# Backward dense stages of a four-layer attention gradient: transposes moved from DMA to TensorE, dq moved, TensorE order set by hand

## The chip, the cores and the metric

The kernel runs on one core of a Trainium2 chip. The metric is the device time of one execution in microseconds, as the median of several executions. Profiles are of one execution each; the two main ones span 3151.3 us (before) and 2894.6 us (after).

## The reference

Forward and gradient of four layers, A B A B, on x of 2048 tokens by 640. A is linear attention with 32 heads of 20; B is softmax attention over a sliding window of 256. Every layer is `x + layer(layernorm(x))`. Outputs: the result, the gradient of x, and the gradients of the four weights (two layers share each).

```python
def _A_ref(x, wqkv, wo):
    q, k, v = split(x @ wqkv)                     # 32 heads of 20
    pq, pk = phi(q), phi(k)                       # where(t > 0, t + 1, exp(t)) + 1e-6
    kv = einsum("bhsd,bhse->bhde", pk, v); z = sum(pk over s)
    return merge(einsum(pq, kv) / (einsum(pq, z) + 1e-6)) @ wo
def _B_ref(x, wqkv, wo):
    p = softmax(mask(q k^T * 20**-0.5))           # 0 <= i - j < 256
    return merge(p v) @ wo
_out, _vjp = jax.vjp(_f, A_x, A_wqkv, A_wo, B_wqkv, B_wo)
return (_out, *_vjp(grad_out))
```
(Names shortened, cuts not marked one by one.)

## The kernel before

The program goes through these stages: forward; dO of layer 3 ("first stage"); attention backward of layer 3; B-to-A (gradient through layer 3's wqkv and layernorm, then dO of layer 2); A-to-B (dq, dk, dv of layer 2, its wqkv and layernorm, then dO of layer 1); attention backward of layer 1; B-to-A and A-to-B again for layers 1 and 0; weight gradients. Tokens go in 16 tiles of 128. `dh` is the large product of a tile (30 matmuls of 320 columns in two halves). The names: `car` holds the gradient of x, `gT` is its transposed tile, which the dO product multiplies with `WoT`; `dqkvT` (after the change `dqT` and `dkvT`) is the transposed gradient of q, k and v, which `dh` multiplies with `WT`; `dNT`, `vT` and `pkT` are the transposed tiles from which dq, dk and dv are made, with small block matrices such as `mbdT`; `dOT` is the transposed output of the dO product for attention. Each product needs its left operand transposed, and before the change nearly all those transposes were DMA transposes issued from SyncE:

```python
def tr(self, out, in_):
    self.nc.sync.dma_start_transpose(out=out, in_=in_)

def load_gT(self, l, tt, pw):
    gT = pw.tile([P, self.DT, P], BF, name="gT")
    self.tr(gT, self.car[:, tt, :])               # car: the gradient of x, all tiles
    self.dma(self.g_d[l][:, tt, :], self.car[:, tt, :])
    return gT

def seg_A_to_B(self, l, acc, dNT):
    ...
    for tt in range(self.TT + 2):
        if tt < self.TT:
            dq[tt] = pw.tile([P, self.QT], BF, name="dqkv_t", bufs=3)
            self.A_dqkv(l, tt, dNT, mats, dq[tt], pw, pps)
        t = tt - 1
        if 0 <= t < self.TT:
            dT = pw.tile([P, self.QTT, P], BF, name="dqkvT")
            self.tr(dT, dq[t])
            self.dma(self.dqkv_d[l][:, t, :], dq.pop(t))
            self.dh(l, t, dT, WT, pw, pps)        # updates car[t]
            ...
        t = tt - 2
        if l > 0 and 0 <= t < self.TT:
            gT = self.load_gT(l - 1, t, pw)
            self.B_do(l - 1, t, gT, WoT, ...)
```

The builder orders each engine's instructions itself, starting from the order of the program; inside `manual_schedule` it keeps the program's order on the engines that are named. Before the change only attention backward did that.

The softmax here doesn't subtract the row's maximum and nothing guards it: scores larger than these inputs give would overflow.

## Time and profile before

| | before |
|---|---|
| median, all its runs beside the change | 3141.5 us (3125.9 to 3158.7, 4 runs); 3156.4 us when the prediction was made |
| five dense stages, with their starts and ends | 1022 us |
| the two attention backwards | 394 + 412 us |
| forward, weight gradients | 902 us, 421 us |

The first part of the page: busy time of each engine and its share of the span. No engine is near full over the whole.

```profile
PE 2248.5 (71%) x22944; PEld 1197.3 (38%) x22944; DVE 1383.5 (44%) x2994; ACT 1066.0 (34%) x2009; POOL 773.2 (25%) x1290
```

Windows cut the span into stretches. The columns are: start and end, length, busy time (and count) of TensorE's matmuls, of its weight loads, of VectorE, ScalarE and GpSimd, the granted TensorE clock, the DMA engines' share, GB/s. I cut at the first and last instruction of `dh` in each dense stage. These are, in order: the first stage, the start of B-to-A (from the last matmul of attention to the first dh), the loop of B-to-A, its end with the start of A-to-B, the loop of layer 2, and, for layer 0, the loop and the step to the weight gradients.

```profile
core 0: us, PE busy (x) PEld busy (x) DVE busy (x) ACT busy (x) POOL busy (x), PEclk, DMA share, GB/s
902.30:1009.60 107.30, 37.29 (x166) 19.71 (x167) 47.26 (x129) 0.00 (x0) 11.40 (x19) 0.63 0.96 213
1403.40:1444.40 41.00, 0.29 (x12) 0.13 (x4) 0.00 (x0) 0.37 (x1) 7.96 (x13) 0.50 1.01 221
1444.40:1586.30 141.90, 106.61 (x739) 72.55 (x739) 91.25 (x229) 16.35 (x62) 25.73 (x55) 0.86 0.62 130
1586.30:1648.60 62.30, 14.00 (x108) 8.08 (x106) 17.32 (x47) 2.03 (x6) 12.39 (x16) 0.61 0.86 174
1648.60:1842.50 193.90, 144.41 (x927) 87.20 (x928) 117.95 (x338) 26.44 (x89) 28.27 (x52) 0.82 0.98 213
...
2530.40:2690.80 160.40, 116.11 (x787) 71.08 (x788) 80.03 (x233) 26.90 (x90) 24.01 (x38) 0.83 0.80 169
2690.80:2730.40 39.60, 0.32 (x3) 0.02 (x1) 2.69 (x7) 0.53 (x2) 0.00 (x0) 0.56 1.13 194
```

TensorE is busy for 107 of 142 us in the loop of B-to-A and 116 of 160 us in layer 0, at a clock of 0.83 to 0.86, while ScalarE is busy for only 16 and 27 us of them. The DMA engines are busy nearly all the time in the first stage and in layer 2 (0.96 and 0.98), not in B-to-A (0.62).

Who TensorE waited for in the loop of layer 2, and then in that of layer 0 (total us, times, longest):

```profile
PE d L565 <- DMA dqkvT<-dqkv_t: 32.6, 6, 12.7
PE d L516 <- DMA gT<-car: 26.3, 7, 6.8
```
```profile
PE d L565 <- DMA dqkvT<-dqkv_t: 60.4, 9, 16.1
```

The chain of waits through layer 0, in order of time (start, length, what; L565 is dh):

```profile
2562.44 9.59 DMA dqkvT<-dqkv_t
2572.07 3.17 PE d L565 x12
2575.24 9.76 DMA dqkvT<-dqkv_t
2585.05 6.63 PE d L565 x30
2593.41 0.58 PE d L622 x9
```

The chain alternates between a DMA transpose of 7 to 16 us and the product that it feeds. Thirty matmuls right after such a wait take up to 6.6 us. Without a wait before them they take 4.1 to 4.2.

### The profile page before, as it was taken

Reading aid. Unit: us, or ns where it says so; the run is one execution under the profiler, and the core shown is the slowest. Engines: PE = TensorE matmul, PEld = TensorE weight load, DVE = VectorE, ACT = ScalarE, POOL = GpSimd, SP = SyncE. Lnnn points to the kernel's source line nnn. Section 1 sums busy time; section 2 is a strip of 40 time slices with the busy share of each in tenths; the row PEclk is TensorE's granted clock in tenths of the full one; section 3 lists DMA queues with packets and bytes.
Section 4 is the critical chain, followed back from the end, with each engine's and each line's share of the span. In section 5 each row is a group of like instructions: output and inputs, shape, how many; then the busy total and the mean of one; then the engine's idle time right before and its main releaser. Section 6 shows DMA issues by size and latency. Waiting matters only on the chain. (4 is left out here: it accounts for less than half of the span.)

```text
span 3151.3 us, 57835 instructions
## 1 busy us (share of the span) xinstructions
PE 2248.5 (71%) x22944; PEld 1197.3 (38%) x22944; DVE 1383.5 (44%) x2994; ACT 1066.0 (34%) x2009; POOL 773.2 (25%) x1290
## 2 busy tenths in 40 slices
PE   7598986699862977774737648776937466497796
PEld 5345544355431322233524423222324344244344
DVE  6344544344233765553736646565726445100000
ACT  4166764277621655540101116554601011000000
POOL 0134442255431433331211113332312111000000
PEclk9789987798755555557868865555568678798898
DMA  6789873989769999998679979999986688954624
GB/s 202 209 161 192 177 176 86 201 180 177 178 162 234 244 201 195 202 185 158 135 162 210 228 197 219 209 194 182 189 169 144 150 162 175 192 119 148 222 78 147
DMA packets 1195024, 563.54 MB, mean 179 GB/s; under 512 B 1036544, under 2 KB 1157376, under 8 KB 1193728
## 3 DMA queue, kind: packets, MB, share of 16 engines
q1 hardware_dynamic: 927488, 245.73, 49.2%
q10 hardware_dynamic: 252544, 261.66, 28.4%
q0 software_dynamic: 14720, 52.44, 6.4%
q8 instruction: 180, 2.95, 0.4%
q14 instruction: 92, 0.75, 0.1%
HBM read 178.65 MB, written 151.13 MB: 105 GB/s over the span
## 5 line engine op out<-in xcount | busy, mean ns | idle before, releaser
L732 DVE TENSOR_TENSOR ds<-sp,e 128x768 bf16<-128x768 f32 (+2 forms) x512 | 460.4, 907 | 319.6 <-PE sp L699 268.5
L713 ACT ACTIVATE e<-sp 128x768 bf16<-128x768 f32 (+2 forms) x512 | 390.2, 774 | 301.7 <-PE sp L699 283.1
L344 ACT ACTIVATE e<-s 128x768 bf16<-128x768 f32 (+2 forms) x512 | 374.0, 774 | 142.2 <-PE s L342 95.9
L565 PEld LDWEIGHTS <-dqkvT 128*128 128x128 bf16 x1920 | 205.8, 109 | 285.5 <-DMA dqkvT<-dqkv_t 99.1
L699 PE MATMUL sp<-KT,QT 32*128 32x384 bf16 (+2 forms) x1024 | 242.6, 477 | 84.0 <-ACT e L713 29.7
L717 POOL TENSOR_SCALAR_AFFINE_SELECT e<-e 128x512 bf16<-128x512 bf16 x256 | 162.5, 635 | 546.3 <-ACT e L713 296.1
L699 PE MATMUL sp<-VT,dOT 32*128 32x384 bf16 (+2 forms) x1024 | 245.1, 470 | 45.9 <-DVE ds L732 29.1
L347 POOL TENSOR_SCALAR_AFFINE_SELECT e<-e 128x512 bf16<-128x512 bf16 x256 | 162.7, 636 | 410.0 <-ACT e L344 371.0
L567 ACT ACTIVATE dh_junk<-d 128x320 bf16<-128x320 f32 x128 | 55.9, 437 | 564.5 <-PE d L565 553.5
L895 DVE CAST wg_r<-wg 128x480 bf16<-128x480 f32 (+1 forms) x36 | 21.7, 602 | 432.3 <-PE wg L891 432.3
L342 PE MATMUL s<-ring 32*128 32x128 bf16 x2880 | 167.9, 236 | 25.6 <-ACT e L344 24.2
L774 PE MATMUL acc<-dsT,ksl 128*32 128x128 bf16 x2880 | 125.8, 305 | 81.3 <-DMA dsT<-ds 79.7
L897 ACT CAST wg_r<-wg 128x480 bf16<-128x480 f32 (+1 forms) x24 | 12.3, 514 | 440.0 <-PE wg L891 440.0
L516 PEld LDWEIGHTS <-gT 128*128 128x128 bf16 x640 | 71.2, 117 | 208.5 <-DMA gT<-car 160.5
L350 POOL TENSOR_SCALAR_AFFINE_SELECT e<-e 128x512 bf16<-128x512 bf16 x224 | 143.3, 640 | 0.0
L721 POOL TENSOR_SCALAR_AFFINE_SELECT e<-e 128x512 bf16<-128x512 bf16 x224 | 142.2, 635 | 0.0
L342 PEld LDWEIGHTS <-ring 32*128 32x128 bf16 x2880 | 83.9, 98 | 134.6 <-issue 127.7
L699 PEld LDWEIGHTS <-dOT 32*128 32x128 bf16 x1024 | 77.7, 99 | 150.1 <-issue 145.4
L699 PEld LDWEIGHTS <-QT 32*128 32x128 bf16 x1024 | 54.8, 100 | 203.6 <-issue 201.4
L216 PEld LDWEIGHTS <-ln_hnT 128*128 128x128 bf16 x960 | 95.9, 106 | 93.0 <-DMA ln_hnT<-ln_hn 36.2
L203 DVE TENSOR_TENSOR car<-d,car 128x320 bf16<-128x320 f32 x128 | 62.2, 486 | 156.7 <-PE d L201 156.0
L363 PEld LDWEIGHTS <-e 128*128 128x128 bf16 x2880 | 103.5, 98 | 67.0 <-POOL e L350 37.9
(587 smaller groups left out, 4076.2 us busy)
## 6 DMA issues: line engine op xcount, KB each, us to landing
qkvT_128<-ring ACTq DMA_DIRECT2D x16, 768.0 KB
qkvT_132<-ring ACTq DMA_DIRECT2D x16, 768.0 KB
dqkvT_118<-dqkvT_g SPq DMA_DIRECT2D x96, 80.0 KB
dqkvT<-dqkvT_118 POOLq DMA_DIRECT2D x4, 1920.0 KB, 18.7
dqkv_116<-dqkv_t ACTq DMA_DIRECT2D x16, 480.0 KB
dqkvT_117<-dqkvT_g SPq DMA_DIRECT2D x96, 80.0 KB
dqkvT<-dqkvT_117 POOLq DMA_DIRECT2D x4, 1920.0 KB, 17.0
dqkv_115<-dqkv_t ACTq DMA_DIRECT2D x16, 480.0 KB
```

Of the source, the lines that this page charges most:

```text
L342: nc.tensor.matmul(ps[:, j, i * P:(i + 1) * P], lhsT=ring[r0:r0 + HP, G + g, kt * P:(kt + 1) * P], rhs=ring[r0:r0 + HP, g, qs], start=True ...
L344: nc.scalar.activation(ev[:, 2 * half:2 * half + 2], ps[:, :, 0:nkt * P].rearrange("p h (i q) -> p h i q", q=P), ACT.Exp, scale=self.c_att)
L347: nc.gpsimd.affine_select(out=ev[:, :, nkt - 1, :], in_=ev[:, :, nkt - 1, :], compare_op=ALU.is_ge, fill=0.0, base=0, pattern=[[0, 4], [1, ...
L350: nc.gpsimd.affine_select(out=ev[:, :, 0, :], in_=ev[:, :, 0, :], compare_op=ALU.is_ge, fill=0.0, base=-1, pattern=[[0, 4], [-1, P]], chan ...
L363: nc.tensor.matmul(ov[:, (g % 4) * 4 + hh, :], lhsT=ev[:, hh, i, :], rhs=slabs[(k0 + i) % len(slabs)][:, c0:c0 + DH + 1], start=(i == 0), ...
L565: nc.tensor.matmul(ps, lhsT=dT[:, k, :], rhs=WT[:, k, cs], start=(k == 0), stop=(k == self.QTT - 1))
L699: nc.tensor.matmul(ps[:, j, 0:nkt * P], lhsT=slabs[g][ta][r0:r0 + HP, b * P:(b + 1) * P], rhs=slabs[g][tb][r0:r0 + HP, k0 * P:(k0 + nkt) * P],
L713: nc.scalar.activation(ev[:, 2 * half:2 * half + 2], ps[:, :, 0:nkt * P].rearrange("p h (i k) -> p h i k", k=P), ACT.Exp, scale=c_att)
L717: nc.gpsimd.affine_select(out=ev[:, :, nkt - 1, :], in_=ev[:, :, nkt - 1, :], compare_op=ALU.is_ge, fill=0.0, base=0, pattern=[[0, 4], [-1 ...
L721: nc.gpsimd.affine_select(out=ev[:, :, 0, :], in_=ev[:, :, 0, :], compare_op=ALU.is_ge, fill=0.0, base=-1, pattern=[[0, 4], [1, P]], chann ...
L732: nc.vector.tensor_tensor(out=dv[:, hs], in0=ps[:, :, 0:nkt * P].rearrange("p h (i k) -> p h i k", k=P), in1=ev[:, hs], op=ALU.mult)
L774: nc.tensor.matmul(acc[HP * hh:HP * (hh + 1), j * P:(j + 1) * P], lhsT=tok("k", g, k0 + i, hh), rhs=dsT[:, hh * nkt + i, :], start=(i == 0 ...
```

## The change

The intent: take the DMA transposes out of the loops by making them on TensorE (matmul with the identity into PSUM, then one ScalarE copy for up to eight blocks); move dq of the A layers from A-to-B to B-to-A, beside its dO; take work off VectorE (t2 to ScalarE, the product for do_s to GpSimd, the slab scaling folded into rinv); issue stores from SyncE; and set TensorE's order by hand so that each transpose stands whole tiles, or half a tile's dh, away from what it waits for. The core of the diff, with cuts marked:

```diff
+    def flip(self, out, blocks, pps):
+        nc = self.nc
+        n = len(blocks)
+        tp = pps.tile([P, 8 * P], BF, name="d")
+        for i, b in enumerate(blocks):
+            nc.tensor.transpose(tp[:, i * P:(i + 1) * P], b, self.ident)
+        nc.scalar.copy(out, tp[:, 0:n * P].rearrange("p (k t) -> p k t", t=P))
...
-        nc.vector.tensor_mul(t, dst, o)
+        nc.gpsimd.tensor_mul(self.hv(t), dst, self.hv(o))
...
-        nc.vector.tensor_scalar(out=t2, in0=hn, scalar1=ab[:, 1:2], scalar2=ab[:, 0:1], op0=ALU.mult, op1=ALU.add)
+        nc.scalar.activation(t2, hn, ACT.Identity, bias=ab[:, 0:1], scale=ab[:, 1:2])
...
     def seg_B_to_A
+            self.dma(mbdT, self.sv[la]["mbdT"])
+            st.enter_context(self.tc.manual_schedule(engines={mybir.EngineType.PE}))
...                                     # dh(i,0), flip g(i-1), dh(i,1), flip dN(i-2), dO(i-1), dq(i-2), flip dq(i-3)
     def seg_A_to_B
+            st.enter_context(self.tc.manual_schedule(engines={mybir.EngineType.PE}))
+            for i in range(-2, TT + 1):
+                    self.dh(l, t, 0, dTs, WT, S, pw, pps)                       # t = i
+                    gT[t] = self.flip_g(l - 1, t, pw, pps)                      # t = i - 1
+                    dkv[t] = self.A_dkv(l, t, lds.pop(t), mats, pw, pps)        # t = i + 1
+                    self.dh(l, t, 1, dTs, WT, S, pw, pps)                       # t = i
+                        self.flip(dkvT[t][:, h * DT:(h + 1) * DT, :], ...)      # t = i + 1, two of them
+                    lds[t] = self.A_loads(l, t, pw, pps)                        # t = i + 2, flips pk
+                    self.B_flip(l - 1, t, pps)                                  # t = i - 2
+                    self.B_do(l - 1, t, gT.pop(t), WoT, pw, pps)                # t = i - 1
```

The transposed weights WT and WoT at the start of each stage, and vT, stay DMA transposes.

## The prediction

> **What bounds the kernel now.** No engine does over the whole span: the first part of the page has TensorE busy 71%, VectorE 44%, ScalarE 34%. I cut the span of 3151 us into stages with the windows view. The change touches five backward dense stages, 934 us in all: dO of layer 3 (77 us), B-to-A (192 us, twice), A-to-B for layer 2 (262 us) and layer 0 (211 us). Forward (905 us), both attention backwards (426 and 430 us) and weight gradients (456 us) keep their code. In those five stages the chain of waits alternates between TensorE and DMA transposes: gT<-car 2.7 to 9 us a wait, dqkvT<-dqkv_t 7 to 16 us a wait. In sum TensorE idles for them 62 us in layer 0, 62 us in layer 2, 41 and 36 us in B-to-A, 37 us in the first stage. ScalarE is nearly idle there (17 us of 192, 29 us of 262). The granted clock is 0.68 to 0.79. A run of 30 dh matmuls takes 4.2 us when TensorE has been kept going, 5.5 to 6.6 us just after such a wait; the Trainium skill ("TensorE: Matmul & The Clock Gate", The HAM clock gate) says that an idle window halves the clock, and these durations agree.
>
> **What changes.** Removed: nearly all per-tile DMA transposes but vT (1.2 us of issue each, 5 us for dqkvT, 2.7 us or more to land), those of dmbdT, one pq reload, and a VectorE pass each for t2 (0.60 us), do_o (0.82) and the slab scaling (0.32). Added: TensorE transposes of 128x128, which I estimate at 0.06 us each at full clock from the 0.064 us of the block-diagonal matmuls of similar width: 16 a tile in B-to-A, 28 in layer 2, 15 in layer 0, 13 in the first stage. Each group needs a ScalarE copy; from 437 ns for 320 and 774 ns for 768 elements I estimate 0.68 us for 640 and 0.97 us for 1024. dq moves into B-to-A (about 0.75 us TensorE and 0.97 us VectorE a tile), which is already full.
>
> Work per tile at full clock, estimated (TensorE / VectorE / ScalarE), against the present pace:
> - first: 2.1 / 2.3 / 1.7 us; now 4.1; expected 3.0
> - B-to-A: 8.2 / 7.0 / 4.2; now 9.4; expected 9.2
> - A-to-B layer 2: 8.3 / 7.0 / 6.9; now 14.1; expected 9.8
> - A-to-B layer 0: 6.2 / 4.8 / 5.0; now 10.1; expected 8.0
>
> **On the critical path.** Times 16 tiles: about 18 + 2x3 + 69 + 34 = 127 us. The start of each A-to-B stage (30 and 48 us) loses the dmbdT transposes: 10 us each; the WT load stays. Starts of B-to-A (41 us wait for WT) stay. Sum 147 us, and 9 more for a warmer clock: **3000 us**, 2930 to 3065 eight times in ten. Faster by over 2%: 0.88; within 2%: 0.10; slower: 0.02.
>
> **What would show it.** Windows: B-to-A near 185 us, layer 2 near 185, layer 0 near 165, first stage near 55; the others within 5 us of now. Waits: gT and dqkvT gone from TensorE's list, shorter ones on ScalarE copies instead. Granted clock above 0.85 in these stages. ScalarE busy more than doubled there.
>
> **What would make it wrong.** The hand-made order is strict: dh of the next tile needs the dkvT copies; if ScalarE does t2 or other copies first, TensorE stalls 2 us or more a tile in layer 0. Stores moved to SyncE wait in order ahead of vT's transposes, which could starve dkv. GpSimd's do_o multiply lies between TensorE and the slab flip. If the transposes don't hold the clock up (same page, PE-mode transpose: they don't count as busy; untested here), the first stage gains little. If none bites, 2930.

## The result, and the profile after

The change takes 2896.6 us (2870.6 to 2898.1, 4 runs), against 3141.5 us: a ratio of 0.920, 95% interval 0.912 to 0.928. A ratio here is the mean time of one kernel's fast runs over that of the other's of the same rounds, so not quite the ratio of the medians. The direction was right; the time lies well below the predicted range (2930 to 3065), and the gain was 245 us, not 156.

The same windows after (the first stage; start and loop of B-to-A; its end with the start of A-to-B; loop of layer 2; then layer 0 and the step to the weight gradients):

```profile
908.80:978.10 69.30, 40.36 (x370) 29.54 (x369) 45.47 (x81) 26.98 (x32) 35.20 (x37) 0.82 0.73 198
1392.60:1433.40 40.80, 0.40 (x13) 0.23 (x6) 1.68 (x2) 0.37 (x1) 13.63 (x20) 0.50 1.00 246
1433.40:1553.80 120.40, 117.04 (x1057) 83.20 (x1057) 91.76 (x239) 55.33 (x117) 42.30 (x54) 0.98 0.40 129
1553.80:1596.00 42.20, 22.51 (x193) 16.23 (x192) 14.84 (x40) 12.93 (x21) 14.30 (x15) 0.66 0.57 132
1596.00:1727.80 131.80, 128.99 (x1231) 95.33 (x1229) 93.78 (x251) 87.81 (x181) 41.59 (x55) 0.99 0.65 177
...
2351.00:2448.90 97.90, 97.88 (x913) 70.49 (x910) 61.42 (x181) 65.54 (x153) 14.56 (x27) 0.99 0.51 146
2448.90:2473.10 24.20, 0.25 (x3) 0.03 (x2) 2.14 (x7) 1.45 (x3) 0.00 (x0) 0.62 1.03 323
```

In the three loops TensorE is now busy 97 to 100% of the time at a clock of 0.98 or more. It is the bound, and it has hardly a gap. The lists of waits say the same: in the loops of B-to-A they hold, beside the wait for WT before the first dh, 3.2 and 3.9 us for VectorE; in the loop of layer 0 TensorE's list is empty, and in that of layer 2 it holds one line:

```profile
PE d L144 <- DVE car L596: 2.6, 3, 1.2
```

The chain through layer 0 is TensorE alone (L614 products with the block matrices, L581 dh, L144 the transposes), 6.23 us a tile:

```profile
2366.94 0.58 PE d L614 x9
2367.52 2.04 PE d L581 x15
2369.56 0.84 PE d L144 x15
2370.40 2.04 PE d L581 x15
2373.17 0.58 PE d L614 x9
```

The first dh half starts at 2367.52 here and again at 2373.75: that is the tile time. The 15 transposes take 0.84 us, 0.056 us each. ScalarE did fit its copies in between; the third line below is both copies of dkvT, and t2 (L595) comes after them, which was the order that the prediction had doubted:

```profile
2394.58 0.44 ACT L583 ACTIVATE dh_junk<-d 128x320 bf16<-128x320 f32 x1 [1.50 <-PE d L581]
2394.91 0.19 ACT L583 ACTIVATION_READ_ACCUMULATOR dh_junk<-d 128x1 f32 x1
2395.00 1.28 ACT L145 COPY dkvT<-d 128x640 bf16<-128x640 bf16 x2
2396.16 0.72 ACT L145 COPY pkT<-d 128x640 bf16<-128x640 bf16 x1
2396.74 0.95 ACT L595 ACTIVATE dh_t_35695<-hn_ld,dh_ab 128x640 f32<-128x640 bf16 x1
```

In B-to-A the chain shows the start of each tile's dO product (L538):

```profile
2242.53 1.36 PE d L538 x10
...
2249.86 1.36 PE d L538 x10
...
2264.71 1.36 PE d L538 x10
...
2273.80 1.36 PE d L538 x10
```

A tile takes 7.33 us (2242.53 to 2249.86), and 9.09 us where the band products of four tiles stand in it (2264.71 to 2273.80), so these cost 1.76 us in four tiles.

What remains in the dense stages is at their starts. TensorE's list over the whole execution still has WT, which comes by DMA transpose:

```profile
PE d L581 <- DMA WT_32780<-in_B_wqkv_dram: 40.8, 1, 40.8
PE d L581 <- DMA WT_21469<-in_B_wqkv_dram: 40.4, 1, 40.4
```

Where the time went, in us, by the two profiles (cut at the same TensorE instructions in both; "A-to-B" counts to the first matmul of the stage after it):

| part | before | after | gained | predicted gain |
|---|---|---|---|---|
| first stage | 107.3 | 69.3 | 38 | 18 |
| starts of B-to-A (two) | 85.7 | 82.0 | 4 | 0 |
| loops of B-to-A (two) | 278.9 | 242.1 | 37 | 6 |
| ends of B-to-A with starts of A-to-B (two) | 123.3 | 81.6 | 42 | 20 |
| layer 2, loop and end | 227.1 | 157.4 | 70 | 69 |
| layer 0, loop | 160.4 | 97.9 | 63 | 34 |
| layer 0 to the first weight-gradient matmul | 39.6 | 24.2 | 15 | 0 |
| sum of these | 1022.3 | 754.5 | 268 | 147 |

Forward, attention and weight gradients together are 11 us longer in this one profile. Attention backward of layer 3 alone lay anywhere between 379 and 415 us in the fast profiles (424 in a slow one), in kernels whose attention code is the same, so single profiles are compared by the dense stages, and whole times by the medians. The predicted gains add to 147 us; the prediction then took 9 more for a warmer clock.

### The profile page after: what moved, and what is told of

It is laid out like the page before. It is cut to its first block, busy times and chain, and to the rows that moved or that the text cites. A ratio compares the mean times of both kernels' runs of the same rounds, so it can differ in the third digit from the quotient of the medians.

```text
span 2894.6 us, 60635 instructions
## 1 busy us (share of the span) xinstructions
PE 2261.8 (78%) x24412; PEld 1255.8 (43%) x24412; DVE 1335.5 (46%) x2804; ACT 1297.4 (45%) x2339; POOL 852.0 (29%) x1310
## 5 line engine op out<-in xcount | busy, mean ns | idle before, releaser
L731 PE MATMUL sp<-KT,QT 32*128 32x384 bf16 (+2 forms) x1024 | 243.1, 477 | 57.7 <-ACT e L745 28.9
L581 PEld LDWEIGHTS <-dqkvT 128*128 128x128 bf16 x960 | 93.1, 100 | 116.4 <-issue 81.6
L806 PEld LDWEIGHTS <-ksl 128*32 128x32 bf16 x2880 | 61.9, 121 | 163.1 <-issue 112.0
## 6 DMA issues: line engine op xcount, KB each, us to landing
dqkvT<-dqkvT_117 POOLq DMA_DIRECT2D x4, 1920.0 KB, 14.1
```

What stands on the lines that cost most here:

```text
L581: nc.tensor.matmul(ps, lhsT=dT[k], rhs=WT[:, k, cs], start=(k == 0), stop=(k == self.QTT - 1))
L731: nc.tensor.matmul(ps[:, j, 0:nkt * P], lhsT=slabs[g][ta][r0:r0 + HP, b * P:(b + 1) * P], rhs=slabs[g][tb][r0:r0 + HP, k0 * P:(k0 + nkt) * P],
L806: nc.tensor.matmul(acc[HP * hh:HP * (hh + 1), j * P:(j + 1) * P], lhsT=tok("k", g, k0 + i, hh), rhs=dsT[:, hh * nkt + i, :], start=(i == 0 ...
```

## The experiments

In what follows, "sum" is the sum of the dense stages as in the table (before 1022, after 754.5). Each run is also a median with a ratio to the kernel before, measured on the same chip in the same rounds. A "flip" is one call of the helper of that name. A "lag" is the number of tiles between a transpose and its use in the order of the program. Experiments 5, 7, 8 and h1 of 11 were measured in rounds where three of the seven runs of the kernel before were slow; the record classes them as "unclear", so their ratios, from fast runs alone, are less sure than their profiles. Different experiments ran on different chips, so two experiments are compared through their ratios and their stages. Every kernel gave correct results.

### 1. Stores from ScalarE (a control)

```diff
     def st(self, out, in_):
-        self.dma(out, in_, self.nc.sync)
+        self.dma(out, in_, self.nc.scalar)
```

> The changed kernel with its per-tile stores issued from ScalarE instead of SyncE (a control for the next run). Theory (TensorE bounds the dense stages, 98% busy there): ScalarE pays some 0.3 us of issue per store, two to four stores a tile, and has 25 to 40% slack, so nothing changes: 2885 to 2925 us. Rival (moving the stores off ScalarE was itself a part of the gain): over 2950 us.

Measured: 2907.1 us, ratio 0.921 (0.914 to 0.928); sum 784. The whole time doesn't tell this from the changed kernel. The profile shows a cost of some 30 us in the sum: the loop of layer 2, where ScalarE is fullest, took 143.6 us and not 131.8, the first stage 77 us and not 69. Where the stores are issued is not what gained, and experiments 2, 4, 5 and 6 use ScalarE for them; their sums are best read against this 784.

### 2. DMA transposes, order by hand

```diff
     def flip(self, out, blocks, pps):
-        (transposes into PSUM, copy)
+        self.tr(out, blocks.src)                  # one DMA transpose; stores from ScalarE
```

> The changed kernel, order by hand and lags kept, but every flip is a DMA transpose from SyncE again, stores on ScalarE as in the kernel before. Theory 1 (the DMA transposes themselves cost: their latency and their share of the DMA queues starve TensorE): most of the gain goes, 3020 to 3130 us, layer-2 A-to-B above 190 us from first dh to last, DMA share there near 1. Rival (the lags of whole tiles would have hidden the DMA transposes just as well): under 2940 us.

Measured: 3177.5 us, ratio 1.004 (0.997 to 1.011, one of its four runs was slow and is left out); sum 1035. All of the gain is gone, and more than theory 1 allowed. TensorE waits for gT, dkvT and dNT; in layer 0:

```profile
PE d L583 <- DMA dkvT<-dkv_t: 48.6, 17, 4.2
```

The DMA share in B-to-A's loop was 0.68 and in layer 2's 0.77, so the queues were not full: what I had called "latency and share of the queues" looked like latency.

### 3. TensorE transposes, automatic order

```diff
-            st.enter_context(self.tc.manual_schedule(engines={mybir.EngineType.PE}))   # in the dense stages
```

> The changed kernel with TensorE's order in the five dense stages left to the scheduler; transposes stay on TensorE. Theory 1 (transposes by DMA were the cost, the order is a small part): 2890 to 2950 us. Rival (the order by hand is what made TensorE run without a gap): 3000 us or more, with TensorE waiting for ScalarE copies and the clock under 0.9.

Measured: 2891.7 us, ratio 0.918 (0.911 to 0.926); sum 759. No loop differs from the changed kernel's by more than 1 us. The automatic order, from the same program, runs without gaps too; the order by hand gained nothing here. The program that the builder starts from still has the lags, so this doesn't show what it would make of a program without them.

### 4. DMA transposes, automatic order

Both edits together (stores from ScalarE).

> DMA transposes and automatic order, the rest of the change (dq beside dO, t2 on ScalarE, do_o on GpSimd, five slabs) kept. If these two parts are all of the gain, this is the kernel before again, 3110 to 3160 us. If moving work off VectorE and dq gained by itself, 3050 us or less.

Measured: 3152.8 us over four runs, of which two were slow (the profiled one too), ratio of the fast ones 0.991 (0.985 to 0.998). Run 6 has the same code but for buffers and a fast profile, with a sum of 999. So with DMA transposes the rest of the change (dq moved, less work on VectorE, the new order of the program) is worth at most about 1% (0.991 here, 0.999 in experiment 6), some 23 us of the sum, and the transposes nearly all of the rest. The strict order even costs here: layer 0's loop took 131 us in this run, with the automatic order, and 167 us in experiment 2. Since this profile is of a slow run, that 131 is read beside the 138 of run 6.

### 5. DMA transposes, order by hand, one more tile of lag

```diff
-                if 0 <= i - 1 < TT:
-                    self.B_do(l, i - 1, gT.pop(i - 1), WoT, pw, pps)
+                if 0 <= i - 2 < TT:
+                    self.B_do(l, i - 2, gT.pop(i - 2), WoT, pw, pps)
...   # the same for dNT, dq, dkvT, pkT, vT and dOT: each used a tile or more later; their buffers 2 -> 3 or 4
```

> As e1_dma_flips (order by hand, DMA transposes), with one more tile of lag between each flip and its use (gT, dNT, dq, dkvT, pkT, vT, dOT) and the buffers for it. If only the latency of the DMA transposes costs, this brings the dense stages close to the changed kernel: B-to-A about 125 us from first dh to last, layer 0 about 105, and 2910 to 2980 us in all. If their throughput costs too (SyncE issues them one after another, 1.2 to 5 us each), layer 2 stays above 165 us and the sum at 3000 to 3080 us. If the order has nothing to do with it, 3140 us or more.

Measured: 2952.9 us, ratio 0.938 (0.931 to 0.945); sum 822. DMA transposes alone, given another tile between issue and use, get 200 of the 268 us. By stage, loop and end together, in us (the control of experiment 1 has the stores where this run has them):

| | before | after | stores from ScalarE (1) | DMA, by hand (2) | DMA, more lag (5) |
|---|---|---|---|---|---|
| first stage | 107 | 69 | 77 | 101 | 95 |
| B-to-A, layers 3 to 2 | 204 | 163 | 169 | 203 | 166 |
| B-to-A, layers 1 to 0 | 198 | 161 | 163 | 202 | 160 |
| A-to-B, layer 2 | 227 | 157 | 169 | 255 | 192 |
| A-to-B, layer 0 | 200 | 122 | 123 | 192 | 127 |

In B-to-A and layer 0 the deeper lag does as well as TensorE transposes, within about 5 us: there only latency cost. In layer 2 and in the first stage it does not; against the control 23 and 18 us are left. TensorE still waits for DMA transposes in the loop of layer 2:

```profile
PE d L540 <- DMA gT<-car: 18.7, 8, 5.4
PE d L583 <- DMA dkvT<-dkv_t: 14.9, 5, 5.9
```

The two windows of this run (first stage, loop of layer 2) have a DMA share of 1.02 and 1.05:

```profile
909.10:1003.90 94.80, 34.22 (x162) 18.19 (x161) 35.02 (x81) 0.00 (x0) 35.12 (x37) 0.64 1.02 217
1607.70:1760.60 152.90, 116.15 (x808) 73.12 (x806) 82.02 (x234) 37.99 (x104) 38.79 (x52) 0.89 1.05 221
```

By the ranges set before the run, latency alone wins: the whole time lies in its 2910 to 2980 us, and the loop of layer 2 is below the 165 us that the second theory asked for. I put what is left in layer 2 and in the first stage down to throughput, but that is argued and not shown. No run gave those stages still more lag. Nor do the traces say whose throughput it would be: the DMA engines' or that of SyncE's queue, which was at DMA transposes for 134 of the 153 us in layer 2. And the DMA share alone doesn't decide it, since the loop of layer 0 had 0.95 in this run, and that stage is within 4 us of the control.

### 6. DMA transposes, automatic order, four buffers

Experiment 4 with `bufs=4` for gT, dNT, dq_t, dkv_t, dkvT, pk_l, pkT, vT and the slopes: was it the buffers of experiment 5 and not its lags?

> As e12_dma_auto (DMA transposes, automatic order), with four buffers instead of two for each tile that a flip reads or writes. The deeper lags of e7_more_lag came with more buffers; this asks whether the buffers alone did it. If the scheduler was only short of buffers: five dense stages under 880 us and 2960 to 3030 us in all. If the lags in the order were what hid the DMA transposes: within 30 us of e12_dma_auto, 3110 to 3170 us.

Measured: 3140.6 us, ratio 0.999 (0.992 to 1.005); sum 999. Buffers alone do nothing with the automatic order, the only one they were tried with. The lag has to be in the order.

### 7. TensorE transposes, by hand, no lag

```diff
+                    self.dh(l, i, 0, ...); self.dh(l, i, 1, ...)
+                    gT[t] = self.flip_g(la, t, pw, pps)
+                    s = self.do_scaled(la, t, gT.pop(t), WoT, ...)
+                    self.flip(dNT[t], ...); dq[t] = self.A_dq(la, t, ...); self.flip(dqT..., dq.pop(t))
...   # all of tile i, then tile i + 1; the first stage and A-to-B likewise
```

> The changed kernel, TensorE transposes, order by hand but with no lag: every flip stands just before its use. The automatic order was as good as the lags; this asks whether slack between producer and consumer is needed at all. If the TensorE transposes are short enough to stand in line, under 2980 us. If the strict order makes TensorE wait out each chain (VectorE, GpSimd, ScalarE, about 8 us a tile), B-to-A takes 250 us or more from first dh to last and the whole 3200 to 3500 us.

Measured: 3608 us, ratio 1.145 (1.133 to 1.156). The window of the loop of B-to-A:

```profile
1495.70:1818.80 323.10, 196.89 (x1110) 114.94 (x1109) 99.18 (x248) 62.96 (x122) 44.40 (x55) 0.71 0.16 49
```

It is 2.7 times as long for the same work, at a clock of 0.71, and the whole is above the 3200 to 3500 us that I had expected. TensorE's longest waits are now for VectorE, before the transposes of car (184 us) and of the dO slabs (112 us). Layer 0, with shorter chains, loses little: its loop takes 117 us against 98. Against the same strict order with lags it costs some 700 us (3608 against 2897). So the lags are needed once the order is strict; given the lags, the strict order is no gain over the automatic one (experiment 3).

### 8. Copies on VectorE

```diff
-        nc.scalar.copy(out, tp[:, 0:n * P]...)
+        nc.vector.tensor_copy(out, tp[:, 0:n * P]...)
```

> The changed kernel with the copies of the flips on VectorE. VectorE is busy 94 of 132 us in layer 2 and 92 of 121 us in B-to-A; the copies bring it some 75 us more in layer 2 and 33 us in each B-to-A, so it would become the bound in layer 2 (near 170 us) and just about in B-to-A (near 125): 2930 to 2990 us. If VectorE copies these bf16 tiles faster than ScalarE (0.69 us for 640), less; under 2910 us would say that the engine of the copies doesn't matter.

Measured: 2910.2 us, ratio 0.924 (0.916 to 0.933); sum 775. That is below the range I gave, and 0.5% above the changed kernel in the ratio, which the intervals do not separate. VectorE copies 640 columns in 0.49 us where ScalarE takes 0.69 us; layer 2's loop and the first stage each grew by 7 us only, to 138.9 and 76.0 us. ScalarE is a good place for the copies, not a necessary one.

### 9. dq back in A-to-B

dNT kept for all tiles, pq loaded again, dq made beside dk and dv, a third flip behind dh. The load of mbdT, which dq needs, moves with it from the start of B-to-A to that of A-to-B.

> The changed kernel with dq of the A layers moved back from B-to-A to A-to-B (dNT of all tiles kept, pq loaded again); transposes and order by hand stay. TensorE bounds both stages, so the same work in another place: each B-to-A about 14 us shorter, each A-to-B about 16 us longer (0.86 to 1.0 us a tile), the whole within 15 us of the changed kernel, 2885 to 2920 us. If the move was itself a gain (it fills otherwise idle TensorE time), 2930 us or more.

Measured: 2915.9 us, ratio 0.928 (0.921 to 0.934); sum 777. The whole is in the range of the first theory, but in three places it differs from what either said. The loops of B-to-A got 4.7 and 5.5 us shorter only (in the first of them TensorE then waited 12.1 us for VectorE's `car`, against 3.2 with dq there, so dq had in part filled time in which TensorE would have waited); layer 0's loop got 43 us longer and not 16; and the starts of B-to-A fell from 41 to 26 us. Layer 0 shows the stall that the prediction had feared, once a tile:

```profile
2366.89 0.44 PE L144 MATMUL d<-ident,pk_l 128*128 128x128 bf16 x5
2368.66 0.58 PE L581 MATMUL d<-WT,dkvT 128*128 128x320 bf16 x3 [1.33 <-ACT dkvT L145]
```

With dq done earlier, the first five of dh's 15 matmuls need only dqT, which is old, and cover the copies of dkvT. With three fresh flips straight before dh, and the one that dh reads first flipped last, nothing covers them; 15 such waits are 20.2 us in that loop. Of the 43 us, 16 are the moved work, as in layer 2 (147.6 against 131.8), and the waits are most of the rest. Without the starts of B-to-A the sum would be 52 us above the changed kernel's; the starts take 29 of them back. Why those got shorter is the question of 12 and 13.

### 10. Do transposes hold the clock?

Before the forward: 400 transposes, 400 matmuls of the same shape, 400 transposes, nothing else on TensorE.

> The changed kernel with a probe at its start: 400 TensorE transposes, 400 matmuls and 400 transposes of the same 128x128 tile, back to back, nothing else on TensorE. If transposes don't hold the granted clock up, [...]both blocks of transposes run at about 0.107 us each (half clock) and only the matmuls reach about 0.056 us. If they count like matmuls, the first block speeds up to about 0.056 us after a few us and stays there through all 1200.

Measured (one profile; the whole takes 2978.3 us with the probe in front). Timeline of TensorE:

```profile
7.17 24.12 PE L426 MATMUL prb_t<-ident,bmask 128*128 128x128 bf16 x400 [7.17 <-POOL ident masks.py:199]
31.13 22.50 PE L424 MATMUL prb_m<-ident,bmask 128*128 128x128 bf16 x400
53.46 22.50 PE L426 MATMUL prb_t<-ident,bmask 128*128 128x128 bf16 x400
```

In the first block the starts are at first 0.107 us apart and after about 3.5 us 0.056 us apart, and they stay so to the end: 400 matmuls take 22.5 us, and so do 400 transposes. The record of the granted clock has full speed from 10.6 us on, 3.5 us after the first transpose and long before the first matmul. Here transposes raised and held the granted clock like matmuls.

### 11. Weights transposed on TensorE: two versions

h1 loads W in five row blocks and flips it in all four stages; h2 does so for B's wqkv alone, with buffers late in memory, and cuts the first load of dqkvT in halves.

```diff
+    def flip_w(self, t, w, n, pool, pps):
+        for kt in range(self.DT):
+            raw = pool.tile([P, n * P], BF, name="w_raw", bufs=5)
+            self.dma(raw, w[kt * P:(kt + 1) * P, :])
+            for a in range(0, n, 8): ...
+                self.flip(t[:, a:z, kt * P:(kt + 1) * P], self.cols(raw[:, a * P:z * P], z - a), pps)
```

> The changed kernel with the transposed weights of the dense stages made on TensorE too: plain loads of W in five row blocks, 75 (or 25) transposes and ScalarE copies, in place of DMA transposes of the whole weight, for which TensorE waits 41 us at the start of each B-to-A. If that wait is the DMA transpose itself, the two starts of B-to-A fall from 41 to 24 to 30 us and those of A-to-B by 5 to 10 us: 2840 to 2870 us. If the start is bound by the dqkvT load or by the stores before it, nothing changes: 2885 us or more.

Measured h1: 2893.8 us, ratio 0.919 (0.911 to 0.926); the starts of B-to-A 40.1 and 39.0 us. Nothing gained, and the ends of B-to-A with the starts of A-to-B, which were to lose 5 to 10 us each, grew from 42 to 51 and from 39 to 45 us. I read the trace so: the loads of the row blocks waited for buffers that attention still held, and dh stood behind the flips of Wo in the same queue (the last of them start at 2187.0 us, dh at 2187.5).

> The changed kernel with two edits at the start of each B-to-A: B's transposed weight made on TensorE from plain loads whose buffers lie late in SBUF, and the first load of dqkvT cut in two halves. h1_w_by_pe gained nothing there because its loads waited for buffers and dh waited for the flips of Wo. If these two waits were the bound, the starts of B-to-A fall from 41 to 25 to 32 us each, 2860 to 2882 us. If the store and reload of dqkvT bound the start, it stays within 5 us: 2885 to 2900 us.

Measured h2: 2869.9 us (2850.4 to 2883.1, 6 runs), ratio 0.911 (0.907 to 0.916); the starts of B-to-A 28.6 and 28.9 us. It changes the buffers, Wo and the first load of dqkvT at once, so which of them was needed is not shown.

### 12. The load of mbdT behind the weight transposes

```diff
-            self.dma(mbdT, self.sv[la]["mbdT"])   # from ScalarE, beside the transpose of WT
+            self.st(mbdT, self.sv[la]["mbdT"])    # from SyncE, issued after WT and WoT
```

> The changed kernel with one edit: the plain load of mbdT (983 KB) at the start of B-to-A is issued from SyncE behind the two weight transposes instead of from ScalarE beside them. In e3_dq_back, which has no such load there, the transpose of WT took 9 us on SyncE's queue and not 16 to 26, and the start of B-to-A 26 us and not 41. If the plain load beside the DMA transpose is the cause: both starts fall to 24 to 30 us, and the whole to 2862 to 2880 us. If something else that moving dq changed is the cause (buffers, the larger dNT): the starts stay at 38 to 42 us and the whole at 2885 to 2900 us.

Measured: 2867.3 us (2856.9 to 2879.2, 6 runs), ratio 0.912 (0.908 to 0.915); sum 730; the starts 26.6 and 28.6 us. SyncE's queue in the second B-to-A, first in the changed kernel, then in this run (start, us on the queue):

```profile
2158.34 25.85 SPq L136 DMA_TRANSPOSE WT_32780<-in_B_wqkv_dram  x1
2184.24 6.17 SPq L136 DMA_TRANSPOSE WoT_32782<-in_A_wo_dram  x1
```
```profile
2143.88 9.66 SPq L136 DMA_TRANSPOSE WT<-in_B_wqkv_dram  x1
2153.59 16.70 SPq L136 DMA_TRANSPOSE WoT<-in_A_wo_dram  x1
2170.33 0.60 SPq L127 DMA_DIRECT2D mbdT<-mbdT  x1
```

The same transpose takes 9.7 us on the queue with mbdT's load (983 KB) behind it, and 25.9 us with that load beside it; at the first B-to-A it is 8.9 against 15.7 us. It was 32.9 us in the kernel before, where the load of dqkvT was issued half a microsecond after it. In this run WoT has dqkvT's load beside it and takes the long time in WT's place, but dh doesn't need WoT.

The DMA packets in the traces show that mbdT's load is not itself what stretches the transpose. WT moves in 9600 packets of 256 bytes. In the changed kernel they start only as mbdT's load ends, 3.8 us after the issue; some 6900 are through when the loads of dqkvT (3.9 MB in packets of 4 KB) begin, only 2100 more get through in the 19 us of those loads, and WT is complete at 2189.1 us, 31 us after its issue. In this run some 9440 are through when the loads of dqkvT begin. So the load that stretches WT is dqkvT's, in the kernel before as well (3900 packets through when it began); mbdT's load only pushed WT's tail into it. TensorE's wait at this start is now for dqkvT:

```profile
PE d L581 <- DMA dqkvT<-dqkvT: 28.3, 1, 28.3
```

It is one line, and the starts become as short as with h2.

### 13. And the first load of dqkvT in halves

> h3_mbdt_behind with the first load of dqkvT cut in two halves. If after h3's edit the load of dqkvT is what the first dh waits for: the starts fall by a further 4 to 8 us each, to 18 to 24 us, 2850 to 2872 us in all. If the WT transpose still is: the same as h3 within 2 us a start.

Measured: 2863.3 us (2848.0 to 2884.5, 6 runs), ratio 0.911 (0.906 to 0.916); sum 726; the starts 23.9 and 27.1 us. The gain over 12 at the starts is 1.5 to 2.7 us, below the 4 to 8 that I expected, and the whole times don't separate the two. TensorE still waits for dqkvT there. Runs 11 (h2), 12 and 13 all beat the kernel before. That they beat the changed kernel too is likely (ratios 0.911 to 0.912 against 0.920, sums 23 to 28 us lower), but the intervals of the ratios touch, and they were not run beside it; 12 needs the least code.

## Why the prediction was wrong, point by point

- **The mechanism was right.** DMA transposes in the loops left TensorE idle; moved to TensorE they did not (experiments 2 to 4: with DMA transposes at the lags of the change the ratio is 0.99 to 1.00, with TensorE transposes 0.92, in either order). gT and dqkvT left TensorE's list, ScalarE's busy time more than doubled there, and the clock rose from 0.82 to 0.86 to 0.98 and more.
- **The step that failed: the pace per tile that was "expected" above TensorE's own work.** I worked out the right bound for layer 0, 6.2 us of TensorE a tile (measured 6.23), and then expected 8.0. The prediction doesn't itemise the 1.8 us between them; what it names is waits on ScalarE's copies and a clock of only "above 0.85". There were no such waits, and the clock was 0.99. That term was 34 us and measured 63. In B-to-A I expected 9.2 us above a bound of 8.2. The prediction counts from the first dh to the last dO product, over 16 tiles; so counted the changed kernel takes 8.1 us (8.07 and 8.15), the bound again. (The steady pace in the chain is lower, 7.33 us and 0.44 for the band products, as the last tiles' work then falls outside.) That term was 6 us and measured 37. The stall was not an invention: it appears at 1.33 us a tile once three fresh flips stand before dh (experiment 9). The order in the change leaves old operands first, and I had not checked for that.
- **The second step: starts and ends of stages**, 20 us predicted and 61 us measured outside the first stage (42 for the ends of B-to-A with the starts of A-to-B, 15 before the weight gradients, 4 before B-to-A). The first stage's 38 us is 21 us in its loop (from the first dO matmul to the last, 67.4 to 46.3 us), close to the 18 predicted, and 17 us at its edges: its window had been cut at 982 us, before the last transposes and stores had landed, and attention began only at 1009.6 us.
- **Layer 2 was right in sum** (69 predicted, 70 measured), in part by luck: the pace of 14.1 us came from a window that begins 19 us before the first dh. From the first dh to the last dO product it was 13.1 us a tile, and it became 8.8, not 9.8; both paces were about 1 us too high, and their difference was right. The loop alone is bound by TensorE at 8.5 us a tile, against 8.3 worked out.
- **"Starts of B-to-A stay" held** (41 us each), but the WT transpose, the reason that I gave, need not take so long: it lay beside the loads of dqkvT in both kernels, in the changed one because mbdT's load, which the change put there, went first. Experiment 12 shows the part of mbdT's load by moving it; that dqkvT's loads do the rest is read from the packets.
- **The order by hand was not needed.** I had treated it as a risk. It was neither a gain nor a loss with TensorE transposes, and a loss with DMA transposes at the same lags.
- **The worry that transposes don't hold the clock up** was unfounded (experiment 10).
- **Stores on SyncE starving vT** did not happen: vT is in no list of waits of the loops after (once, for 5.5 us, before the first dh of layer 2), and stores from ScalarE were no better.

What stays open: why the step from layer 0 to the weight gradients lost 15 us. It did so with DMA transposes too (24 to 25 us in experiments 2 and 6), so TensorE transposes are not the cause. The first transpose there, of dqkvT, has plain loads of hn beside it, and took 33 us on the queue before and 17 us after, which may be the same as in experiment 12. But it was not tested. The spread of attention's time between executions is not explained either.

## What to carry to other kernels

Work out what the fullest engine must do per tile, and if the operands that the next product reads first are a tile old, expect that bound itself and not a stall above it; look for the order of operands before adding an allowance. The cost of a DMA transpose in a loop was for the most part latency here: more lag in the order cured it, more buffers alone did not. What a deeper lag leaves may be throughput; try the lag first and see which stages stay behind. At the start of a stage put the loads that are needed late behind the DMA transpose that is needed first, and look at what large load its tail will meet.

## What the Trainium skill lacked or had wrong

- "TensorE: Matmul & The Clock Gate", PE-mode transpose, says that the full clock doesn't engage for transposes, which don't count as PE-busy in the same way. Here 400 transposes alone brought the clock up within about 3.5 us and then ran 0.056 us apart, exactly as matmuls do (experiment 10). The same section gives about 390 ns for one transpose in isolation and about 275 ns in one kernel; here the record of one is 219 ns long, and in a row one costs 0.056 us.
- The same page, The HAM clock gate, says that an idle window takes the clock to half. This agrees: after a wait the dh matmuls of the kernel before start 0.267 us apart at a granted clock of 0.50, and 0.136 us apart once it is 1.00, so that thirty take up to 6.6 us and not 4.1.
- "VectorE: DVE Perf Modes", The three transpose paths, gives 1309 ns for a DMA transpose and 390 ns on TensorE. That is right in direction, but it is for one block. In these loops a DMA transpose stood in the chain of waits for 2.7 to 8.5 us where it had 5 blocks (gT) and for 7 to 16 us where it had 15 (dqkvT).
- "Advanced Engine Details and Errata", X-Bar Transpose (TRN2), says that transpose DMAs are as fast as regular DMAs, and expects 350 to 400 GB/s. With almost no load beside it, WT (640x1920 of two bytes, 2.46 MB) moved in 9.2 us at the first B-to-A of experiment 12, about 267 GB/s, and a plain load, mbdT, moved 983 KB in 3.3 us in the changed kernel, about 298 GB/s: the two are near each other, and both are below the page's figure. Beside the loads of dqkvT WT took 31.5 us from issue to the first dh in the changed kernel: about 78 GB/s.
- No page has a figure for what plain loads cost a large DMA transpose that runs beside them: during the 19 us of dqkvT's loads 2100 of WT's packets got through in the changed kernel, against some 9400 in 9 to 10 us without such a load (experiment 12).
